# Four scheduling edits in the attention layers of a four-layer transformer block: residual rows by pairs of tiles, the mask row written from another queue, later mask copies, an earlier v tile

## The chip, the cores and the metric

The kernel runs on one core of a Trainium2 chip. A core has a matrix engine (TensorE, PE in the profile, with its weight loads listed apart as PEld), three engines for elementwise work (VectorE or DVE, ScalarE or ACT, GpSimd or POOL) and SyncE (SP), which here only issues DMA transfers. Each engine works through its own instructions in order. PE writes its results to PSUM, from where DVE or ACT has to bring them to the on-chip SBUF; DMA transfers move data between SBUF and device memory, and here also between partitions of SBUF. A DMA is issued from an engine's queue and occupies that engine for the time of the issue only, but an issue can wait for a semaphore, and everything behind it on that engine waits with it.

The metric is device time in microseconds (us) of one launch on this core: the median of several runs.

## The reference

Four layers, A, B, A, B, on an input of 2048 rows of 576 bf16 values; each adds its result to its input.

```python
def _A_ref(x, wqkv, wo):            # D=576, H=32 heads, Dh=18
    W, dil = (8, 2)
    q, k, v = split_heads(x @ wqkv)
    idx = pos[:, None] - (arange(W) * dil)[None, :]      # 8 keys: own row, 2 back, ... 14 back
    logits = einsum('bhsd,bhswd->bhsw', q, k[idx]) * Dh ** -0.5
    logits = where(idx >= 0, logits, -1e9)
    o = einsum('bhsw,bhswd->bhsd', softmax(logits), v[idx])
    return merge_heads(o) @ wo

def _B_ref(x, w_in, w_sp, b_sp, w_out):                  # F=4608
    z = gelu(x @ w_in)
    z1, z2 = z[..., :2304], layernorm(z[..., 2304:])
    g = einsum('ts,bsf->btf', w_sp, z2) + b_sp           # w_sp: 2048 x 2048
    return einsum('bsf,fd->bsd', z1 * g, w_out)

x = x + _A_ref(layernorm(x), A_wqkv, A_wo)
x = x + _B_ref(layernorm(x), B_w_in, B_w_sp, B_b_sp, B_w_out)
...
```

The two lines are run twice, with the same weights.

## The kernel before

**Layout.** The normalised input is kept transposed in `xnT` (features on partitions, 5 pieces of 128, the last one half filled). Queries and keys are wanted with each head on its own 18 partitions of a group of 32: `QK` is 128 partitions (4 heads) x 2 (q and k) x 8 groups x 2064 columns. The 14 partitions that a head leaves free hold the mask: rows of a pattern that repeats every 256 columns, so arranged that the matmul of a key tile with a query tile adds a large negative number wherever a key is not one of the 8 that a query may see. The rows are built once in a small tile (`win_rows`, L123), written to device memory (`win_period`, L174, in the function that the prologue calls as `rows[2]`), read back by four loads into the spread layout (`load_pat`, L176), and copied along the columns by DVE: `fill_window_rows` (L188), four copies of 128x4096 (L197) for each half of 1024 columns.

**Projections.** `VW(t, hh)` (L373) computes half of the v rows of query tile t: five matmuls into a `pv` tile of PSUM and one eviction to `v_ext`. `PG(d, qk, cc)` (L384) computes 128 features of q or k (piece d) for 512 rows (chunk cc): five matmuls into `pp`, one eviction to a staging tile (`stg`, L369 on DVE or L371 on ACT). After the last of the four `PG` of a staging tile (both of q and k, two chunks) come its head moves: 7 to 9 DMAs, one per head, from the staging tile to the partitions of that head in `QK`, dealt in turn to SP and POOL. In the first layer A two of the five staging tiles are lent by `win2a`, a weight tile that is loaded later, so the moves of d=3 and d=4 of the first two chunks appear in the profile as `QK<-win2a`.

**Attention.** A query tile has 112 rows (19 tiles) and is done in two steps of 16 heads (38 steps). `L_mm(s)` (L435): 16 matmuls of 32 rows into two `L_ps` tiles (PSUM tag H, 2 buffers); `EXP(s)` (L444): two exponentials on ACT into `P_sb`; `PV(s)` (L455): 16 matmuls into `O_ps`, then a reciprocal and a multiplication on DVE into `o_t` (L461, L462). After the second step of a tile, SP issues a DMA transpose of `o_t` to `oT` (L467). All of `pv`, `pp`, `O_ps`, `pw` and the transposes `pt` share four PSUM buffers (tag PT).

**Output.** For each of 16 tiles of 128 rows: `XO(i)` (L478) loads the residual rows to `xo`, `WO(i, hh)` (L482) multiplies `oT` by `wo` in two halves (`pw`, L489) and adds `xo` (L492) into `x_new`, `XST` stores it, `LN_STATS` (L500) and `LN_XN` (on POOL, L242 and L245) normalise it for the next layer, `LN_T` has SP transpose it into `xnT`. `xo` has three buffers, `x_new` four.

**Order.** Inside a layer A no scheduler reorders anything: each engine executes its instructions in the order of the code. The loop over steps puts out `L_mm(s+1)`, `EXP(s+1)`, `PV(s)` and then whatever `table` holds for step s: the `PG` of chunks 2 and 3 that are left after six `pre` ones (steps 0 to 12, more than one at some), the v tiles not yet done, weight loads, and the output stages, whose step follows from the tile that they need.

**The opening of the first layer A** is a sequence written out by hand (L572 to L631): `S_` statistics of input tiles on DVE, `E_` adds epsilon to a variance (DVE), `R_` raises it to the power -0.5 (POOL), `A_` normalises (DVE), `T_pe` transposes on PE with a copy on ACT (L567), `T_` transposes by DMA, with `VW` and `PG` between them, then v tiles 4 to 7, the second half of the mask copies, `L_mm(0)`, `EXP(0)` and the six `pre` groups. At its start SP's queue issues the loads of x, `wv`, x, `wqk` (key half, then query half) and x.

The layers B (L714 on) are not touched.

Of the kernel before, what the change touches and what calls it, by code (L numbers as in the profile page):

```python
# [18 lines left out]
P = 128  # L19
D = 576  # L20
# [42 lines left out]
class K:  # L63
# [48 lines left out]
        self.xn_rr = 0  # L112
        self.deferred = []

    def build_window_rows(self, c):

        nc = self.nc
        R = c.tile([P, 2, MR, 16], bf16, name="win_rows")  # L123
        self.pat = self.consts.tile([P, 2, 272], bf16, name="win_pat")
        self.patpad = self.consts.tile([P, PADL], bf16, name="win_patpad")
        n = c.tile([P, 3], i32, name="win_n")
        g = c.tile([P, 3], i32, name="win_g")
        bits = c.tile([P, 5, 3], i32, name="win_bits")
        vf = c.tile([P, 5, 3], f32, name="win_vf")
        uu = c.tile([P, 4, 2], f32, name="win_uu")  # L130
        half = WB / 2
        nc.gpsimd.iota(n[:], pattern=[[1, 3]], base=15, channel_multiplier=1)
# [12 lines left out]
        nc.gpsimd.memset(R[:, 0, 13, :], -2.5 * WB)  # L145
        nc.gpsimd.memset(R[:, 1, 13, :], 1.0)
        one = self.dram.tile([2, MR, 256], bf16, name="win_period")
        for xb in self.xn_bufs:
            nc.gpsimd.memset(xb[:, D:640], 0.0)

        def part0():
            nc.vector.tensor_scalar(out=n[:], in0=n[:], scalar1=15, scalar2=None, op0=ALU.bitwise_and)
            nc.vector.tensor_scalar(out=g[:], in0=n[:], scalar1=1, scalar2=None, op0=ALU.logical_shift_right)
            nc.vector.tensor_tensor(out=g[:], in0=g[:], in1=n[:], op=ALU.bitwise_xor)
            for i in range(4):
                nc.vector.tensor_scalar(out=bits[:, i, :], in0=g[:], scalar1=i, scalar2=1,
                                        op0=ALU.logical_shift_right, op1=ALU.bitwise_and)
            nc.vector.tensor_scalar(out=bits[:, 4, :], in0=n[:], scalar1=1, scalar2=None, op0=ALU.bitwise_and)

        def pads():  # L160
            nc.gpsimd.memset(self.pat[:], 0.0)
            nc.gpsimd.memset(self.patpad[:], 0.0)
            for j in range(4):
                nc.gpsimd.affine_select(out=self.patpad[:], in_=self.patpad[:], compare_op=ALU.not_equal, fill=1.0,
                                        base=-32 * j - 31, pattern=[[0, PADL]], channel_multiplier=1)

        def part1(eng):
            nc.vector.tensor_scalar(out=vf[:], in0=bits[:], scalar1=-2.0, scalar2=1.0, op0=ALU.mult, op1=ALU.add)
            nc.vector.tensor_scalar_mul(out=R[:, :, 0:8, :], in0=R[:, :, 0:8, :], scalar1=vf[:, 4, 1:2])
# [152 lines left out]
    def layer_A(self, li):  # L322
# [17 lines left out]
        oT = main.tile([P, 5, RING * P], bf16, name="oT")  # L340
        sb_cm = tc.tile_pool(name=f"A{li}_sb", bufs=2, reuse_waits="tile")
        sb = sb_cm.__enter__()
        if self.right is None:
            self.open_right()
        R = self.right
# [130 lines left out]
        tails = {}  # L476

        def XO(i):  # L478
            tails[i] = dict(xo=sb.tile([P, D], x_prev_dt, name="xo", tag="xo", bufs=3))
            self.dma(tails[i]["xo"][:], x_prev[i * P:(i + 1) * P, :], eng=nc.sync)  # L480

        def WO(i, hh):  # L482
            st = tails[i]
            if hh == 0:
                st["x"] = sb.tile([P, D], f32, name="x_new", tag="x_new", bufs=4)
            r0 = (i % RING) * P
            pw = self.PT_tile([P, 512], f32, "pw")
            for c in range(5):
                nc.tensor.matmul(pw[:, 0:288], lhsT=oT[:, c, r0:r0 + P], rhs=wo_sb[:, c, hh * 288:(hh + 1) * 288],  # L489
                                 start=(c == 0), stop=(c == 4))  # L490
            hs = slice(hh * 288, (hh + 1) * 288)
            nc.vector.tensor_tensor(out=st["x"][:, hs], in0=pw[:, 0:288], in1=st["xo"][:, hs], op=ALU.add)  # L492
# [17 lines left out]
        if li == 0:  # L510
# [19 lines left out]
            warm = self.PT_tile([P, 512], f32, "warm")  # L530
            for _ in range(46):
                nc.tensor.matmul(warm[:, 0:P], lhsT=self.ident[:], rhs=self.ident[:], start=True, stop=True)
            rows = self.build_window_rows(sb)
            nc.scalar.copy(out=v_ext[:, :, :, DH:DH + 1], in_=self.ones[:, None, None, :].to_broadcast([P, NT, H, 1]))
            rows[0]()
            mvs = sb.tile([P, NS, 2], f32, name="lnx_mv", tag="lnx_mv", bufs=1)
# [6 lines left out]
                        nc.vector.bn_stats(out=st[:, s, :], in_=xts[i][:, s * 288:(s + 1) * 288])  # L543
                    nc.vector.bn_aggr(out=mvs[:, i, :], in_=st[:])

            def E_(i0, n):
                nc.vector.tensor_scalar_add(out=rstds[:, i0:i0 + n], in0=mvs[:, i0:i0 + n, 1], scalar1=EPS)

            def R_(i0, n):
                nc.gpsimd.tensor_tensor(out=rstds[:, i0:i0 + n], in0=rstds[:, i0:i0 + n],  # L550
                                        in1=self.neg_half[:, 0:1].to_broadcast([P, n]), op=ALU.pow)
            xns = {}

            def A_(*tiles):
# [15 lines left out]
                for i in tiles:  # L570
                    self.ln_T(xns.pop(i), i * P, P)
            S_(0)  # L572
            E_(0, 1)
            R_(0, 1)
            S_(1)
            E_(1, 1)
            R_(1, 1)
            A_(0)
            T_pe(0)
            VW(0, 0, False)  # L580
            VW(0, 1, False)
            S_(2)
            A_(1)
            T_pe(1)
            VW(1, 0, False)
            S_(3)
            E_(2, 2)
            R_(2, 2)
            rows[1]()
            setup_bufs(nc.gpsimd)  # L590
            rows[2](nc.scalar)
            A_(2, 3)
            T_pe(2)
            T_pe(3)
            VW(1, 1, False)
            x_load(sb.tile([P, 4, D], bf16, name="x_in3", tag="x_in", bufs=2)[:], 12, 4, nc.sync)
            S_(4, 5)
            E_(4, 2)
            R_(4, 2)
            VW(2, 0, False)  # L600
            VW(2, 1, False)
# [1 line left out]
            A_(4, 5)  # L603
            T_(4, 5)
            S_(7)
            E_(6, 2)
            R_(6, 2)
            S_(8)
            A_(6, 7)
            T_(6, 7)  # L610
            self.load_pat(nc.sync)
            S_(9, 10, 11)
            E_(8, 4)
            R_(8, 4)
            S_(12)
            A_(8, 9, 10, 11)
            T_(8, 9, 10, 11)
            self.fill_window_rows(QK, 0)
            S_(13, 14, 15)
            E_(12, 4)  # L620
            order = [(d, 0) for d in range(4)] + [(d, 1) for d in range(4)] + [(4, 0), (4, 1)]
            for k_, (d, cc) in enumerate(order):
                for qk in ((1, 0) if d < 4 else (0,)):
# [23 lines left out]
        for t in range(nvw0, nvw):  # L647
            for hh in range(2):
                VW(t, hh, li == 0)
        if li == 0:  # L650
            self.fill_window_rows(QK, 1)

        pieces = []

# [12 lines left out]
        PG_END = 14  # L667
        pre, pgs = pgs[:6], pgs[6:]
        for k_, (d, qk, cc) in enumerate(pgs):
            at((k_ * PG_END) // len(pgs), PG, d, qk, cc, True)  # L670
        for t in range(nvw, NT):
            for hh in range(2):
                at(2 * t - 2 + hh, VW, t, hh, 2 * t - 2 + hh >= PG_END and hh == 0)
        for i in range(NS):
            t = -(-(i + 1) * P // QT) - 1
            s = 2 * t + (6 if li == 0 and t < 8 else 5 if t < NT - 5 else 4 if t < NT - 3 else 3)
            at(s - 5, XO, i)
            at(s, WO, i, 0)
            at(s + 1, WO, i, 1)
            at(s + 1, LN_STATS, i)  # L680
            at(s + 2, LN_XN, i)
            at(s + 2, XST, i)
            if i < NS - 1:
                at(s + 4, LN_T, i)
# [8 lines left out]
        at(NST, O_T, NT - 1)  # L693
        L_mm(0)
        EXP(0)
        for d, qk, cc in pre:
            PG(d, qk, cc, li > 0, q2)
        for s in range(NST):
            if s + 1 < NST:
                L_mm(s + 1)  # L700
# [343 lines left out]
```

The softmax here doesn't subtract the row's maximum and nothing guards it: scores larger than these inputs give would overflow.

## Time and profile before

| what | us |
|---|---|
| median of 6 runs (1193.01 to 1197.96) | 1194.18 |
| the profiled execution, by the same clock as the runs | 1196.53 |
| its span in the profile | 1194.8 |
| PE busy in the span | 1172.7 |
| opening, 0 to 24: PE busy | 18.45 |
| projections of the first layer A, 24 to 50: PE busy of 26 | 24.85 |
| its attention loop, 50 to 118: PE busy of 68 | 63.16 |
| first layer B, 118 to 595: PE busy of 477 | 474.42 |
| projections of the second layer A, 595 to 645: PE busy of 50 | 49.68 |
| its attention loop, 645 to 715: PE busy of 70 | 68.38 |
| second layer B, 715 to 1194.8: PE busy of 479.8 | 473.70 |

The stage borders are mine, to the nearest few us; the busy times are the profile's. The loops are full of small groups. In the first one (50 to 118) they are, with the columns line, engine, operation, output<-inputs, shapes, count, then busy time and mean ns of one, then idle time of the engine ahead of them and what ended it:

```profile
L444 ACT ACTIVATE P_sb<-L_ps 128x896 bf16<-128x896 f32 x59 | 50.6, 916 | 16.2 <-PE L_ps L435 15.8
L455 PE MATMUL O_ps<-v_ext,P_sb 128*128 128x19 bf16 x480 | 16.9, 172 | 0.0
L489 PE MATMUL pw<-wo_sb,oT 128*128 128x288 bf16 x100 | 15.5, 286 | 2.7 <-DMA oT<-o_t 1.9 <-DVE o_t L462 0.8
L400 PE MATMUL pp<-xnT,wqk_sb 128*128 128x512 bf16 x54 | 14.5, 378 | 0.3
```

A row of the order of time gives start, duration, engine, line, operation and names, and in brackets how long the engine was idle before it and what it had waited for; SPq, ACTq and POOL L77 are DMA issues (L77 is the helper that issues them all). Here a stretch of SP's queue in the first loop:

```profile
92.24 0.53 SPq L77 DMA_DIRECT2D xo<-in_A_x_dram  x1
92.86 1.20 SPq L249 DMA_TRANSPOSE xnT<-ln_xn  x1
94.11 0.57 SPq L77 DMA_DIRECT2D xres<-x_new  x1
94.79 1.29 SPq L467 DMA_TRANSPOSE oT<-o_t  x1
96.17 1.51 SPq L249 DMA_TRANSPOSE xnT<-ln_xn  x1
```

A stage's row in the table by windows has the window, its length, the busy time and number of instructions of PE, PEld, DVE, ACT and POOL, the granted TensorE clock (1.00 is full speed), the mean busy share of the 16 DMA engines (it can read above 1), and GB/s.

### The profile page before, as it was taken

The numbers are of one execution on the slowest core, as the hardware profiler recorded it, in microseconds if no ns is written. First come the engines' busy times: TensorE is split into PE (matmuls) and PEld (weight loads), VectorE is DVE, ScalarE is ACT, GpSimd is POOL, SyncE is SP. The second block draws the span as 40 slices with busy tenths as digits, with TensorE's granted clock in tenths as the row PEclk, the third lists the DMA queues.
The fourth block names the chain that finished last, engine by engine and source line by source line (L and its number), as shares of the span: only waits on it lengthen the run. The fifth ranks groups of instructions, "written<-read, shape, count | busy, mean of one in ns | idle before, by whom it ended". The sixth has DMA issues, their size and how long they took to land.

```text
span 1194.8 us, 20693 instructions
## 1 busy us (share of the span) xinstructions
PE 1172.7 (98%) x8457; PEld 620.0 (52%) x8554; DVE 545.4 (46%) x1202; ACT 378.7 (32%) x597; POOL 275.1 (23%) x382
## 2 busy tenths in 40 slices
PE   8999999999999999999999999999999999999998
PEld 5566644444444444457755775444444444444676
DVE  8577677333233233244455776763223223233321
ACT  5577677211111111201156786770110110111000
POOL 3677774100000000001153867630000000000000
PEclk9999999999999999999999999999999999999999
DMA  8799891000000000049645799900000000001332
GB/s 193 146 198 225 167 257 35 23 1 12 12 12 12 12 1 12 2 139 294 170 98 120 172 233 221 199 11 12 12 12 1 12 12 12 12 1 30 122 105 73
DMA packets 178791, 101.21 MB, mean 85 GB/s; under 512 B 135039, under 2 KB 160047, under 8 KB 178696
## 3 DMA queue, kind: packets, MB, share of 16 engines
q1 hardware_dynamic: 165400, 78.14, 29.5%
q0 software_dynamic: 6480, 15.99, 5.1%
q10 hardware_dynamic: 6816, 5.77, 1.6%
q8 instruction: 67, 1.10, 0.4%
q14 instruction: 28, 0.23, 0.1%
HBM read 42.39 MB, written 16.53 MB: 49 GB/s over the span
## 4 chain that ended last, share of the span: by engine, by line
PE 93%; DMA 2%; issue 1%; ACT 0%; DVE 0%; DVEq 0%; ACTq 0%
PE pg L878 41%; PE pz L860 12%; PE po L932 12%; PE pz L782 11%; PE pp L400 4%; PE pw L489 3%; PE O_ps L455 3%; PE pv L377 3%; PE L_ps L435 2%; PE pzs L782 1%; DMA oT<-o_t 1%; ACT P_sb L444 0%; DMA QK<-win2a 0%; PE pt L473 0%; DVE ln_st L218 0%
## 5 line engine op out<-in xcount | busy, mean ns | idle before, releaser
L878 PE MATMUL pg<-Wq,Z 128*128 128x512 bf16 x2256 | 500.3, 379 | 2.5
L878 PEld LDWEIGHTS <-Z 128*128 128x128 bf16 x2304 | 225.5, 98 | 271.7
L882 DVE TENSOR_TENSOR g_tmp<-pg,ln_xn 128x512 f32<-128x512 f32 x144 | 99.6, 692 | 428.1 <-PE pg L878 428.1
L872 ACT ACTIVATE z1T<-pz 128x1024 bf16<-128x1024 f32 x72 | 73.7, 1024 | 513.8 <-PE pz L860 513.6
L77 POOL DMA_DIRECT2D wout<-in_B_w_out_dram x4 | 4.2, 1060 | 604.6 <-PE pg L878 604.6
L932 PE MATMUL po<-wout,Z 128*128 128x288 bf16 x1152 | 141.4, 286 | 0.0
L444 ACT ACTIVATE P_sb<-L_ps 128x896 bf16<-128x896 f32 (+1 forms) x152 | 126.7, 887 | 42.3 <-PE L_ps L435 41.5
L860 PE MATMUL pz<-xnT,w 128*128 128x512 bf16 (+1 forms) x630 | 134.4, 380 | 1.6 <-issue 1.6
L932 PEld LDWEIGHTS <-Z 128*128 128x128 bf16 x1152 | 112.7, 98 | 28.8
L782 PEld LDWEIGHTS <-xnT 128*128 128x128 bf16 (+1 forms) x800 | 66.3, 97 | 80.9 <-issue 23.7
L883 DVE TENSOR_TENSOR Z<-g_tmp,z1T 128x512 bf16<-128x512 f32 x144 | 99.7, 692 | 10.8 <-DVE g_tmp L882 1.4
L782 PE MATMUL pz<-win2a,xnT 128*128 128x512 bf16 x366 | 103.5, 380 | 0.8
L860 PEld LDWEIGHTS <-w 128*128 128x128 bf16 (+1 forms) x640 | 51.1, 97 | 80.0 <-issue 27.1
L400 PE MATMUL pp<-xnT,wqk_sb 128*128 128x512 bf16 x341 | 81.0, 379 | 0.9
L796 ACT ACTIVATE zp<-pz 128x1024 bf16<-128x1024 f32 x64 | 65.5, 1024 | 36.7 <-PE pz L782 34.1
L242 POOL TENSOR_SCALAR ln_xn<-x_new,ln_mv,ln_rstd 128x576 bf16<-128x576 f32 x32 | 73.4, 2293 | 2.7
L942 DVE TENSOR_TENSOR x_new<-po,xo 128x288 f32<-128x288 f32 (+1 forms) x64 | 28.8, 455 | 88.0 <-PE po L932 83.7
L782 PE MATMUL pz<-win2b,xnT 128*128 128x512 bf16 (+1 forms) x256 | 65.8, 380 | 0.0
L798 DVE CUSTOM_DVE_ANT_0 Z<-zp 128x1536 bf16<-128x1536 bf16 x32 | 56.5, 1764 | 15.8 <-ACT zp L796 15.6
L377 PE MATMUL pv<-wv_sb,xnT 128*128 128x288 bf16 (+1 forms) x380 | 56.2, 285 | 3.8 <-ACT xnT L567 3.7
L77 POOL DMA_DIRECT2D QK<-stg x81 | 49.8, 619 | 39.8 <-DVE stg L369 13.4
L489 PE MATMUL pw<-wo_sb,oT 128*128 128x288 bf16 x320 | 48.8, 286 | 3.2 <-DMA oT<-o_t 2.4
(111 smaller groups left out, 873.0 us busy)
## 6 DMA issues: line engine op xcount, KB each, us to landing
xres<-x_new SPq DMA_DIRECT2D x48, 288.0 KB
xo<-xres SPq DMA_DIRECT2D x48, 288.0 KB
wout<-in_B_w_out_dram POOLq DMA_DIRECT2D x4, 1296.0 KB, 8.6
w<-in_B_w_in_dram SPq DMA_DIRECT2D x16, 256.0 KB
QK<-stg POOLq DMA_DIRECT2D x53, 72.0 KB, 4.2
QK<-stg SPq DMA_DIRECT2D x41, 72.0 KB
xo<-in_A_x_dram SPq DMA_DIRECT2D x16, 144.0 KB
win2a<-in_B_w_in_dram POOLq DMA_DIRECT2D x6, 288.0 KB, 4.3
```

The costliest lines, as they stand in the source:

```text
L242: e.tensor_scalar(out=xn[:nrows, 0:D], in0=x_t[:nrows, :], scalar1=mv[:nrows, 0:1], scalar2=rstd[:nrows, 0:1], op0=ALU.subtract, op1=ALU.mult)
L377: nc.tensor.matmul(pv[:nk, 0:288], lhsT=self.xnT[:, c, QT * t:QT * t + nk], rhs=wv_sb[:, c, hh * 288:(hh + 1) * 288], start=(c == 0), stop ...
L400: nc.tensor.matmul(pp[:, :], lhsT=w, rhs=self.xnT[:, c, PADL + cc * 512:PADL + (cc + 1) * 512], start=(c == 0), stop=(c == 4))
L444: nc.scalar.activation(out=P_bufs[(2 * s + jp) % 4][:nk, :, :, 0:nq], in_=Lv[:nk, :, :, 0:nq], func=ACT.Exp, scale=scale)
L489: nc.tensor.matmul(pw[:, 0:288], lhsT=oT[:, c, r0:r0 + P], rhs=wo_sb[:, c, hh * 288:(hh + 1) * 288], start=(c == 0), stop=(c == 4))
L782: nc.tensor.matmul(pzvs[ci][:, sub * 512:sub * 512 + w], lhsT=self.xnT[r0:r1, c, PADL + i * P:PADL + (i + 1) * P], rhs=win2(c)[r0:r1, c0 + ...
L860: nc.tensor.matmul(pz1s[q // 2][:, q % 2, :], lhsT=w1[r0:r1, c, sub * P:(sub + 1) * P], rhs=self.xnT[r0:r1, c, PADL + q * 512:PADL + (q + ...
L872: nc.scalar.activation(out=z1T[:, q2 * 512:(q2 + 2) * 512], in_=pz1s[q2 // 2][:, :, :].rearrange("p a b -> p (a b)"), func=ACT.Gelu_apprx_ ...
L878: nc.tensor.matmul(pg[:, :], lhsT=Z[:, jj, i, sub * P:(sub + 1) * P], rhs=Wq[q][:, i, :], start=(i == 0), stop=(i == NS - 1))
L882: nc.vector.tensor_tensor(out=tmp[:], in0=pg[:, :], in1=bsp[:, qs], op=ALU.add)
L883: nc.vector.tensor_tensor(out=uT(jj)[:, sub, qs], in0=tmp[:], in1=z1Ts[jj, sub][:, qs], op=ALU.mult)
L932: nc.tensor.matmul(acc[hh], lhsT=uT(j // 2)[:, j % 2, i * P:(i + 1) * P], rhs=wouts[j // NJH][:, j % NJH, hh * 288:(hh + 1) * 288], start= ...
```

## The change

1. The residual rows come two tiles at a time: `XO(i)` does nothing for an odd i and loads tiles i and i+1 with one DMA for an even i, at the step at which tile i alone was loaded. `xo` has 2 buffers of two tiles in place of 3 of one. The first two `xo` and all four `x_new` tiles are allocated at the start of the layer.
2. The rows of the mask pattern are built in a part of `oT` that is not in use then, in place of a tile of their own, and the write of the pattern to device memory is issued by POOL instead of ACT.
3. In the opening of the first layer A, `E_` is put out together with `R_`, and the first v tile comes after the transposes of tile 1 instead of before them.
4. In the first layer A the second half of the mask copies comes after the fourth `pre` group instead of before `L_mm(0)`; the first four `pre` groups are evicted by DVE instead of ACT.
5. In the first layer A the twelve remaining `PG` go to steps 2 to 13, one each, instead of steps 0 to 12; v tile 8 goes to steps 0 and 1 (evicted by DVE), instead of 14 and 15; the output stages of the tile that needs query tile 9 (tile 7) come one step later.

```diff
-        R = c.tile([P, 2, MR, 16], bf16, name="win_rows")
...
+        x_news = [sb.tile([P, D], f32, name="x_new", tag="x_new", bufs=4) for k_ in range(4)]
+        xos = {k_: sb.tile([P, 2, D], x_prev_dt, name="xo", tag="xo", bufs=2) for k_ in range(2)}
...
         def XO(i):
-            tails[i] = dict(xo=sb.tile([P, D], x_prev_dt, name="xo", tag="xo", bufs=3))
-            self.dma(tails[i]["xo"][:], x_prev[i * P:(i + 1) * P, :], eng=nc.sync)
+            if i % 2 == 0:
+                xo = xos.pop(i // 2, None) or sb.tile([P, 2, D], x_prev_dt, name="xo", tag="xo", bufs=2)
+                self.dma(xo[:], x_prev[i * P:(i + 2) * P, :].rearrange("(a p) d -> p a d", p=P), eng=nc.sync)
+                for k_ in range(2):
+                    tails[i + k_] = dict(xo=xo[:, k_, :])
...
-            rows = self.build_window_rows(sb)
+            nR = 2 * MR * 16
+            rows = self.build_window_rows(
+                sb, oT[:].rearrange("p a b -> p (a b)")[:, 4 * D:4 * D + nR].rearrange("p (a r f) -> p a r f", a=2, r=MR))
...
-            def E_(i0, n):
-                nc.vector.tensor_scalar_add(out=rstds[:, i0:i0 + n], in0=mvs[:, i0:i0 + n, 1], scalar1=EPS)
-
             def R_(i0, n):
-                nc.gpsimd.tensor_tensor(out=rstds[:, i0:i0 + n], in0=rstds[:, i0:i0 + n],
-                                        in1=self.neg_half[:, 0:1].to_broadcast([P, n]), op=ALU.pow)
+                rs = rstds[:, i0:i0 + n]
+                nc.vector.tensor_scalar_add(out=rs, in0=mvs[:, i0:i0 + n, 1], scalar1=EPS)
+                nc.gpsimd.tensor_tensor(out=rs, in0=rs, in1=self.neg_half[:, 0:1].to_broadcast([P, n]), op=ALU.pow)
...
             T_pe(0)
-            VW(0, 0, False)
-            VW(0, 1, False)
             S_(2)
             A_(1)
             T_pe(1)
+            VW(0, 0, False)
+            VW(0, 1, False)
             VW(1, 0, False)
...
-            rows[2](nc.scalar)
+            rows[2](nc.gpsimd)
...
-        if li == 0:
-            self.fill_window_rows(QK, 1)
...
-            at((k_ * PG_END) // len(pgs), PG, d, qk, cc, True)
+            at(2 + k_ if li == 0 else (k_ * PG_END) // len(pgs), PG, d, qk, cc, True)
         for t in range(nvw, NT):
             for hh in range(2):
-                at(2 * t - 2 + hh, VW, t, hh, 2 * t - 2 + hh >= PG_END and hh == 0)
+                if li == 0 and t == nvw:
+                    at(hh, VW, t, hh, True)
+                else:
+                    at(2 * t - 2 + hh, VW, t, hh, 2 * t - 2 + hh >= PG_END and hh == 0)
...
-            s = 2 * t + (6 if li == 0 and t < 8 else 5 if t < NT - 5 else 4 if t < NT - 3 else 3)
+            s = 2 * t + (6 if li == 0 and t < 10 else 5 if t < NT - 5 else 4 if t < NT - 3 else 3)
...
-        for d, qk, cc in pre:
-            PG(d, qk, cc, li > 0, q2)
+        for k_, (d, qk, cc) in enumerate(pre):
+            PG(d, qk, cc, li > 0 or k_ < 4, q2)
+            if li == 0 and k_ == 3:
+                self.fill_window_rows(QK, 1)
```

More of the change, by code (lines that the diff above doesn't have):

```diff
@@ L113, in setup, with build_window_rows @@
         self.deferred = []
-    def build_window_rows(self, c):
+    def build_window_rows(self, c, R):
         nc = self.nc
-        R = c.tile([P, 2, MR, 16], bf16, name="win_rows")
         self.pat = self.consts.tile([P, 2, 272], bf16, name="win_pat")
@@ L484, in WO @@
             if hh == 0:
-                st["x"] = sb.tile([P, D], f32, name="x_new", tag="x_new", bufs=4)
+                st["x"] = x_news[i] if i < 4 else sb.tile([P, D], f32, name="x_new", tag="x_new", bufs=4)
             r0 = (i % RING) * P
@@ L572, in layer_A @@
             S_(0)
-            E_(0, 1)
             R_(0, 1)
             S_(1)
-            E_(1, 1)
             R_(1, 1)
@@ L584, in layer_A @@
             T_pe(1)
+            VW(0, 0, False)
+            VW(0, 1, False)
             VW(1, 0, False)
             S_(3)
-            E_(2, 2)
             R_(2, 2)
@@ L597, in layer_A @@
             S_(4, 5)
-            E_(4, 2)
             R_(4, 2)
@@ L605, in layer_A @@
             S_(7)
-            E_(6, 2)
             R_(6, 2)
@@ L612, in layer_A @@
             S_(9, 10, 11)
-            E_(8, 4)
             R_(8, 4)
@@ L619, in layer_A @@
             S_(13, 14, 15)
-            E_(12, 4)
             order = [(d, 0) for d in range(4)] + [(d, 1) for d in range(4)] + [(4, 0), (4, 1)]
```

## The prediction

> **What bounds the kernel.** First the page's busy line, then TensorE's waits, then the stages that hold them.
>
> ```profile
> PE 1172.7 (98%) x8457; PEld 620.0 (52%) x8554; DVE 545.4 (46%) x1202; ACT 378.7 (32%) x597; POOL 275.1 (23%) x382
> ...
> PE pv L377 <- ACT xnT L567: 3.7, 3, 2.1
> PE pw L489 <- DMA oT<-o_t: 2.4, 3, 1.4
> PE L_ps L435 <- ACT P_sb L444: 2.2, 6, 0.4
> PE L_ps L435 <- DMA QK<-win2a: 1.5, 3, 0.7
> ```
>
> TensorE is busy all but 22 us, so an edit that takes no matmul away can only win idle time. A wait line gives total, times, longest. The table by stage shows where it lies (us, then PE busy):
>
> ```profile
> 0.00:20.00 20.00, 14.46 (x116) 10.56 (x118) 16.95 (x65) 10.82 (x16) 8.68 (x42) 1.00 0.94 239
> 40.00:60.00 20.00, 18.31 (x236) 9.70 (x239) 12.04 (x21) 13.45 (x18) 9.28 (x12) 1.00 0.79 137
> 100.00:120.00 20.00, 17.02 (x332) 12.20 (x332) 13.63 (x42) 14.62 (x20) 14.55 (x17) 1.00 1.10 238
> 680.00:700.00 20.00, 18.98 (x382) 13.88 (x379) 14.83 (x44) 16.88 (x23) 14.66 (x16) 1.00 1.20 232
> ```
>
> Idle: 5.5 us in the opening, 1.7 where attention begins, 3.0 late in the first layer A, 1.0 in the second. The granted clock is 1.00 throughout.
>
> **Opening.** The order of time on ACT and PE:
>
> ```profile
> 11.02 0.40 ACT L371 CAST v_ext<-pv 128x288 bf16<-128x288 f32 x1 [0.88 <-PE pv L377]
> 13.14 0.33 ACTq L77 DMA_DIRECT2D win_period<-win_rows  x1
> 13.52 1.29 ACT L567 COPY xnT<-pt 128x640 bf16<-128x640 bf16 x2 [2.10 <-DVE lnx_mv L544]
> 14.26 1.40 PE L377 MATMUL pv<-wv_sb,xnT 128*128 128x288 bf16 x10 [2.11 <-ACT xnT L567]
> ```
>
> The copies need only transposes that ended at 11.5; the mask write ahead of them in ACT's queue is what waits. In the built program the transfers of SP and ACT take eight completion counters in turn (POOL's have eight others), and an issue waits until the last transfer on its counter has landed: here the key half of wqk. Moved to POOL, the write holds nobody there: POOL is through with its memsets at 12.34, its next operation (the pow at 13.65) awaits DVE, and its one issue costs 0.6 (head move) to 1.06 (the 1.3 MB wout row). The readers (load_pat, SP, 21.08) are far off. Putting the transposes of tile 1 ahead of the first v tile removes the 0.81 us wait at 10.19 as well, so PE could start wqk 2.1 earlier. But its second group reads the query half. By bytes in queue order, key half (2.36 MB) landed near 13.1, x tiles 8 to 11 (3.76 MB) at 16.88; the query half (3.10 MB) falls at 15.1. PE read it at 16.6. Gain 1.4; bounds 0.3 (SP's second transpose, behind the query half's counter, starts at 16.3) and 2.1.
>
> [...]
>
> **Head moves.** The first attention half needs the moves of d=0, 1 and the first two of d=2, the second (L_mm(1)) the moves of d=3 and 4, which POOL issues last:
>
> ```profile
> 41.35 5.49 POOL L77 DMA_DIRECT2D QK<-win2a  x5 [0.28 <-DMA QK<-stg]
> 41.62 4.62 DVE L197 COPY QK<-win_pat 128x4096 bf16<-128x4096 bf16 x4
> ...
> 50.42 0.09 PEld L435 LDWEIGHTS <-QK 32*128 32x128 bf16 x1 [0.85 <-DMA QK<-win2a]
> ...
> QK<-win2a POOLq DMA_DIRECT2D x1, 72.0 KB, 6.1
> ...
> QK<-win2a POOLq DMA_DIRECT2D x2, 36.0 KB, 4.0
> ```
>
> Five issues take 5.49 us where the median is 0.587, that is 2.94. Singly they end at 42.94, 44.07, 45.21, 46.35 and 46.84; the copies end at 42.84, 43.98, 45.11 and 46.24: each issue comes free 0.1 us after a mask copy. The change puts those four copies behind four pp evictions, at about 46.2. Without them the fifth issue is held by its counter only: the transfer eight before it, issued at 38.73 and 6.1 us on the way, lands at 44.8. POOL's chain (no gap from 28.60 to 41.07) starts with the first stg, up to 1.4 sooner; but half 0's copies run from 24.49 to 29.12 and slow its first two moves to some 1.1 each, so 0.7 is left. Fifth issue 44.1 instead of 46.33; last landing, 4.0 to 4.5 later, 48.1 to 48.6 instead of 50.4. PE comes to L_mm(1) at 46.7 instead of 48.05 and resumes at 48.3 instead of 50.4: **gain 2.1**, the opening's 1.4 included. Bounds: 1.1 (POOL starts no sooner, 4.5 us: 49.3) and 2.9 (landing in 3.4, the least of the five before). SP's moves from 28.58 to 42.0 stay, behind transposes that DVE times.
>
> What the copies now delay: 46.2 + 4.6 = 50.8 for the first reciprocal. Four PSUM buffers cover that; PE needs the first again at PV(2), near 52. If the cover fails, up to 1 us. Four pp evictions of 0.69 go to DVE, four of 0.59 leave ACT: both idle there. Merging E_ with R_ changes no order that anyone awaits; the pow of tiles 12 to 15 stands behind POOL's moves before and after. Storing the rows in oT and allocating tiles early issue nothing.
>
> **Loop of the first layer A.** From one PV to the next I read 1.92 and 2.22 in turn with a pp (mean 2.07), 2.53 with pp and pw, 1.92 with neither, 2.23 with pw alone. Steps 0 to 15 took 35.4 before. After: two with pv (ACT's two P_sb, 1.73, set the pace: 1.85), six with pp, six with both, two with pw (2.1): 35.5. **0**, within 0.4. PG of chunk 3 at step 2 falls near 52, after its transposes (issued by 47.3).
>
> But the last head moves (d=4) now leave at step 13, not 12. PE reaches PV(13) at 77.3 and the eviction ends near 79.8; SP, behind the transpose of o_t 6, issues four moves at 0.78 from about 81.8, the last landing 3.5 later at 88.4; L_mm(19) wants them at 87.5. **Loss 0.9**; bounds 0 (landing in 2.8, the quickest move) and 2.0 (4.5).
>
> **Output tiles.** SP is full from 55 to 118: the transpose of o_t 9, ready at 93.8, is issued at 99.47. So pw waits: 1.39 (tile 7), 0.48, and 0.78 put down to o_t: 2.65 in all. Pair loads drop four xo issues by then, 4 x 0.5 = 2.0 us of SP; its first head moves start 1.2 later. Tile 7 also moves one step (2.1) on. I take the 1.39 and half of the rest as won, 2.0, less 0.7 for a step that loses its pw and becomes ACT's: **gain 1.3**; bounds 0 (the DMA share, 1.10, sets the pace: the bytes are the same) and 2.65.
>
> **Second layer A.** Only pairs (f32) change; no new buffer wait: pair i still waits for add i-3. Two waits, 0.49 (oT) and 0.40 (P_sb, not touched). **Gain 0.2**; bounds +0.5 and -1.2 (288 KB more ahead of one transpose at 240 GB/s).
>
> **Sum.** 2.1 + 0 - 0.9 + 1.3 + 0.2 = 2.7. The profiled execution took 1196.53 (span 1194.8 and 1.73 around it), 2.35 above the median of six: 1193.8 for it, 1191.5 for the median.
>
> **Rivals.** (1) *SP and the DMA engines keep the pace*: what PE wins by 50 us it gives back at L_mm(19) and the pw waits, since the bytes and most issues stay. For it: DMA share 1.10 at 100 to 120. Against: every xo dropped leaves the full queue. Gain 2.1 - 2.0 + 0.6 + 0 = 0.7: 1193.5. (2) *Pair loads in front of transposes*, in the second layer A: an even tile's load of 576 KB stands ahead of an o_t transpose that pw awaits, while the share is 1.2. Price 1.2 each at pairs 8 to 14, 4.8, and the output term falls away: 1194.18 - 1.2 + 4.8 = 1197.8, slower. It eats the whole gain from 0.34 us a pair over eight pairs (2.7 / 8). Against: only one pw wait there now. (3) *The copies are not what slows POOL* but the counters: then the five issues stay, the change does not do what it says, and 0.3 to 1 is left at L_mm(1): 2.7 - 1.5 = 1.2: 1193.0. Against: the ends 0.1 behind each copy.
>
> **Chances.** Forecast 0.55, rivals 0.23 (1), 0.12 (2), 0.10 (3). The forecast's own range is 1189.5 to 1191.8; the whole reaches to rivals 1 and 3 and stops at 1195.0, leaving most of rival 2 and gains above 4.7 out. 0.2% (2.4 us) is about what this kernel's measurement can tell from no change: faster 0.55, same 0.33, slower 0.12.
>
> **What would show it.** Five issues in under 3.6 us before 45; L_mm(1) through by 48.6; no idle PE at 12 to 14; mask copies from 46; a QK wait near 87; pw waits under 1 us in 95 to 115. Wrong if L_mm(1) still ends past 50, or the second layer A shows pw waits above 2.

## The result, and the profile after

The changed kernel takes 1197.30 us (median of 38 runs, 1193.85 to 1200.80); the kernel before, run beside it, 1195.92 (median of 78). The ratio is 1.0013, with a 95% interval of 1.0007 to 1.0019: 1.6 us slower where 2.7 us of gain had been forecast. That is inside the 0.2% that were called no change, and clear of zero on the wrong side. (The profiled execution of one experiment, e5, ran at a granted clock of 0.95 from end to end, so no profile of it is read below.)

The profiled execution took 1197.59 us (span 1195.8). From its page, the busy line and the granted clock in 40 slices:

```profile
PE 1175.2 (98%) x8457; PEld 621.8 (52%) x8554; DVE 547.8 (46%) x1207; ACT 376.0 (31%) x592; POOL 273.5 (23%) x383
...
PEclk9998999999999999999999999999999999999999
```

And TensorE's waits (total, times, longest):

```profile
PE L_ps L436 <- DMA QK<-stg: 4.6, 1, 4.6
PE pw L493 <- issue: 2.4, 2, 1.7
...
PE L_ps L436 <- DMA QK<-win2a: 0.2, 1, 0.2
```

The waits that the change aimed at are nearly gone: no pv waits for `xnT`, `QK<-win2a` is down from 1.5 to 0.2 us, no pw waits for `oT` (not a proof of part 1, as e10 will show). One wait of 4.6 us is new, and PE's busy time is 2.5 us longer although the page lists the same 8457 matmuls: one digit of the granted clock is 8. The table by stage (us, then PE, PEld, DVE, ACT, POOL, clock, DMA share, GB/s) shows where:

```profile
0.00:20.00 20.00, 17.56 (x129) 12.16 (x131) 18.11 (x68) 12.49 (x19) 9.26 (x43) 1.00 1.00 243
40.00:60.00 20.00, 19.58 (x283) 10.65 (x284) 15.52 (x28) 13.76 (x17) 6.00 (x12) 1.00 0.70 137
80.00:100.00 20.00, 13.54 (x235) 9.52 (x232) 9.81 (x29) 9.98 (x14) 13.87 (x17) 0.83 1.16 174
100.00:120.00 20.00, 19.02 (x375) 14.09 (x373) 15.59 (x48) 16.55 (x23) 14.26 (x15) 1.00 1.19 225
```

Idle PE in the opening fell from 5.5 to 2.4 us, where attention begins from 1.7 to 0.4, late in the layer from 3.0 to 1.0, in the second layer A from 1.0 to 0.5. All of it and more is lost between 80 and 100: 6.5 us idle, at a mean clock of 0.83. The order of time on PE there:

```profile
84.35 0.77 PE L378 MATMUL pv<-wv_sb,xnT 128*128 128x288 bf16 x5
84.96 0.29 PE L493 MATMUL pw<-wo_sb,oT 128*128 128x288 bf16 x1
86.98 0.65 PE L493 MATMUL pw<-wo_sb,oT 128*128 128x288 bf16 x4 [1.74 <-issue]
87.56 0.32 PE L436 MATMUL L_ps<-QK 32*128 32x112 bf16 x6
92.50 1.17 PE L436 MATMUL L_ps<-QK 32*128 32x112 bf16 x10 [4.62 <-DMA QK<-stg]
93.60 0.60 PE L456 MATMUL O_ps<-v_ext,P_sb 128*128 128x19 bf16 x16
94.05 1.36 PE L378 MATMUL pv<-wv_sb,xnT 128*128 128x288 bf16 x5
```

In the kernel before, nothing waits there:

```profile
89.83 0.51 PE L435 MATMUL L_ps<-QK 32*128 32x112 bf16 x16
90.27 0.56 PE L455 MATMUL O_ps<-v_ext,P_sb 128*128 128x19 bf16 x16
```

In the changed kernel L_mm(19) starts, finds the last head moves (d=4) missing, and waits. Afterwards the same five pv matmuls take 1.36 us instead of 0.77. Counted by the start of PV, the loop is ahead of the kernel before by 4.0 us at PV(1) (48.48 against 52.50) and by 4.2 at PV(17) (83.93 against 88.09); at PV(18) it is 3.3 us behind (93.60 against 90.27). So one place took 7.5 us: the 4.62, the 1.74 and the slower clock.

The head moves at the start of attention came as forecast, and sooner: L_mm(1) is through at 46.73, where 48.6 was asked for. POOL's last moves, in the order of time (POOL, DVE, PE):

```profile
37.70 3.56 POOL L77 DMA_DIRECT2D QK<-win2a  x6
41.51 1.55 POOL L77 DMA_DIRECT2D QK<-win2a  x3 [0.24 <-DMA QK<-stg]
...
44.38 4.62 DVE L196 COPY QK<-win_pat 128x4096 bf16<-128x4096 bf16 x4
...
46.30 0.43 PE L436 MATMUL L_ps<-QK 32*128 32x112 bf16 x2 [0.18 <-DMA QK<-win2a]
```

Before, five issues took 5.49 us, the first four of them ending 0.1 us behind a mask copy each; now the last three take 1.55, and the copies run behind them.

### The profile page after: what moved, and what is told of

The parts are those of the page before. It is cut to its first block, busy times and chain, and to the rows that moved or that the text cites. A ratio compares the mean times of both kernels' runs of the same rounds, so it can differ in the third digit from the quotient of the medians.

```text
span 1195.8 us, 20663 instructions
## 1 busy us (share of the span) xinstructions
PE 1175.2 (98%) x8457; PEld 621.8 (52%) x8554; DVE 547.8 (46%) x1207; ACT 376.0 (31%) x592; POOL 273.5 (23%) x383
## 4 chain that ended last, share of the span: by engine, by line
PE 95%; DMA 1%; POOL 1%; issue 1%; DVE 1%; ACT 1%; SPq 0%
PE pg L878 41%; PE pz L860 12%; PE po L932 12%; PE pz L782 11%; PE pp L401 5%; PE pw L493 3%; PE pv L378 3%; PE O_ps L456 3%; PE L_ps L436 2%; PE pzs L782 1%; POOL QK L77 1%; DMA QK<-stg 1%; ACT P_sb L445 1%; DMA QK<-win2a 0%; DVE ln_st L549 0%
## 5 line engine op out<-in xcount | busy, mean ns | idle before, releaser
L883 DVE TENSOR_TENSOR Z<-g_tmp,z1T 128x512 bf16<-128x512 f32 x144 | 99.7, 692 | 10.1 <-DVE g_tmp L882 0.5
```

The source lines that it names most:

```text
L883: nc.vector.tensor_tensor(out=uT(jj)[:, sub, qs], in0=tmp[:], in1=z1Ts[jj, sub][:, qs], op=ALU.mult)
```

## The experiments

All ratios are to the kernel before, on the same chip, each with its 95% interval; medians are of 12 runs (5 for e4). Runs of one kernel spread over some 6 us and each kernel has one profile, so a wait read from it is a sample.

**The first question: which part brought the wait?** Part 5 undone, pairs undone, the six weight loads taken out of the stretch, and part 5 alone.

```diff
# e1, against the changed kernel
-            at(2 + k_ if li == 0 else (k_ * PG_END) // len(pgs), PG, d, qk, cc, True)
+            at((k_ * PG_END) // len(pgs), PG, d, qk, cc, True)
-                if li == 0 and t == nvw:
-                    at(hh, VW, t, hh, True)
-                else:
-                    at(2 * t - 2 + hh, VW, ...)
+                at(2 * t - 2 + hh, VW, ...)
-            s = 2 * t + (6 if li == 0 and t < 10 else ...)
+            s = 2 * t + (6 if li == 0 and t < 8 else ...)
```


> The changed kernel with part 5 alone undone (remaining PG at steps 0 to 12 again, v tile 8 at 14 and 15, tile 7's output not shifted). Theory 'late by order': in the changed kernel PE waits 4.62 us at L_mm(19) because the last head moves (d=4) are put out a step later; with the old order they leave 3 to 5 us earlier, the wait falls under 1 us, the granted clock stays at 1.00, and the time falls 5 to 7 us below the changed kernel (about 4 below the kernel before). Rival 'slow moves': the moves are late because they take 11.1 us to land among the weight and residual loads, whatever step puts them out; then the wait stays above 3 us and the time within 1.5 us of the changed kernel.

Measured: 1193.29 us, ratio 0.9977 (0.9965 to 0.9989). No wait for `QK<-stg` at L_mm(19); 4.3 us below the changed kernel by the ratios (0.0036 of 1195.9), somewhat less than the 5 to 7 expected. The rest of the change is a gain, and part 5 eats it.

```diff
# e2, against the changed kernel
             if i % 2 == 0:
                 xo = xos.pop(...)
-                self.dma(xo[:], x_prev[i * P:(i + 2) * P, :].rearrange(...), eng=nc.sync)
                 for k_ in range(2):
                     tails[i + k_] = dict(xo=xo[:, k_, :])
+            self.dma(tails[i]["xo"], x_prev[i * P:(i + 1) * P, :], eng=nc.sync)
```


> The changed kernel with one residual tile per transfer again (two for each pair, at the old steps; the allocation stays). If the 288 KB pair loads ahead of the head moves in SP's queue are what makes them land late, the wait at L_mm(19) falls under 2 us and the time falls by 3 to 6 us. If they are not ('late by order' and 'slow moves' by weights alike), the wait stays within 1 us of 4.62, SP has 8 more issues of 0.5 us in the first layer A, and the time is the changed kernel's or up to 1.5 us more.

Measured: 1197.62 us, ratio 1.0014 (1.0002 to 1.0026), the changed kernel's time. The wait is 3.2 us and 0.4 more, with head moves that land in 5.9 us at the most. Pair loads don't cause it, and landing times as long as the changed kernel's 11.1 us are not needed for it.

```diff
# e3, against the changed kernel
-                at(5 + 2 * k_, f)          # six win2a loads
+                at(k_ // 2, f)
```


> The changed kernel with the six win2a loads (288 KB each, POOL) at steps 0 to 2 in place of 5 to 15: into the stretch 47 to 55, where the DMA share is 0.17 to 0.98, and off the head moves. 'Slow moves': head moves of chunks 2 and 3 land in 5 us or less again (median was 6.7, longest 11.2), no wait above 1 us at L_mm(19), clock 1.00, time 5 to 8 us below the changed kernel. 'Late by order': the last moves still leave at 80 to 84 and the wait stays above 3 us, the time within 1.5 us.

Measured: 1194.34 us, ratio 0.9990 (0.9979 to 1.0001); head moves land in 5.6 us or less (4.2 in the median), and three short waits are left at L_mm(19), 1.4 us in all. Neither expectation fits whole: landing got quicker, the time fell by some 2.8 us, half of what the theory of slow moves asked for.

```diff
# e4: the diff of e1 the other way round, on the kernel before
```


> The kernel before with part 5 alone (PG at steps 2 to 13, v tile 8 at 0 and 1, tile 7's output a step later). 'Late by order': the last moves leave a step later against the same consumer, a wait of 3 to 5 us at L_mm(19), time 4 to 7 us above the kernel before. If the wait needs the earlier start of the loop as well (PE 3.9 us ahead while SP's and POOL's queues are not), the wait is under 1.5 us and the time within 1.5 us of the kernel before.

Measured: 1200.04 us, ratio 1.0036 (1.0024 to 1.0048): 4.3 us slower, with a wait at the same place:

```profile
94.43 1.20 PE L435 MATMUL L_ps<-QK 32*128 32x112 bf16 x10 [4.96 <-DMA QK<-stg]
```

Part 5 needs none of the other edits to do its damage; alone and taken out of the whole it gives the same 4.3 us.

**The second question: what are the parts worth?** e5 and e12 change the changed kernel, e11 the kernel before; the others undo or move one part more in e1.

```diff
# e5, against the changed kernel: PG steps alone undone
-            at(2 + k_ if li == 0 else (k_ * PG_END) // len(pgs), PG, d, qk, cc, True)
+            at((k_ * PG_END) // len(pgs), PG, d, qk, cc, True)
```


> The changed kernel with only the PG of chunks 2 and 3 back at steps 0 to 12; v tile 8 stays at 0 and 1, tile 7's output a step later. If the PG steps are what made part 5 dear (last moves a step, about 2.2 us, later), the wait for QK<-stg at L_mm(19) falls under 1.5 us and the time is within 0.15% of e1 (1193.3), 3 to 5 us below the changed kernel. If moving v tile 8 or the outputs is what costs (two PT users more in the early steps, the later pw ones bunched), the time stays within 1.5 us of the changed kernel.

Measured: 1195.14 us, ratio 0.9995 (0.9984 to 1.0006), 2.2 us below the changed kernel and 2.2 above e1: between the two expectations.

```diff
# e6, against e1
+        if li == 0:
+            self.fill_window_rows(QK, 1)           # before L_mm(0)
...
-            PG(d, qk, cc, li > 0 or k_ < 4, q2)
-            if li == 0 and k_ == 3:
-                self.fill_window_rows(QK, 1)
+            PG(d, qk, cc, li > 0, q2)
```


> e1 with part 4 undone too (mask copies of the second half before L_mm(0) again, all pre groups evicted by ACT). If the copies hold POOL's last five issues, these take 5 us or more again, L_mm(1) ends 1 to 2 us later than in e1, and the time rises by 1.0 to 2.0 us. If POOL's issues are held by the counters anyway, the time stays within 0.6 us of e1.

Measured: 1194.40 us, ratio 0.9994 (0.9984 to 1.0005), 2.0 us above e1. POOL's last nine issues in e6, in the order of time:

```profile
37.73 7.62 POOL L77 DMA_DIRECT2D QK<-win2a  x9
```

And in e1:

```profile
37.85 1.17 POOL L77 DMA_DIRECT2D QK<-win2a  x2
39.34 0.59 POOL L77 DMA_DIRECT2D QK<-win2a  x1 [0.32 <-DMA QK<-stg]
40.95 0.59 POOL L77 DMA_DIRECT2D QK<-win2a  x1 [1.01 <-DMA QK<-stg]
41.69 2.81 POOL L77 DMA_DIRECT2D QK<-win2a  x5 [0.16 <-issue]
```

Nine take 7.62 us behind the copies; without them the issues are 0.6 us each and what holds them is, as forecast, the landing of an earlier transfer. Even so POOL is through at 44.5 in e1 and at 45.4 in e6: the copies cost 0.9 us at POOL, and L_mm(1) ends 1.0 us later (PV(0) starts at 48.79 instead of 47.77).

```diff
# e7, against e1
-            rows[2](nc.gpsimd)
+            rows[2](nc.scalar)
# and the two calls VW(0, 0), VW(0, 1) again right behind T_pe(0)
```


> e1 with the opening undone (mask write from ACT again, first v tile before the transposes of tile 1). If the write waits for the key half of wqk in every execution, as in the trace of before (2.1 us of idle PE), the time rises by 1.4 to 2.7 us. If that wait depends on when the load lands (in e4, with the same opening, the write left at 11.12 without waiting), the trace shows it in some runs only, and the time rises by 0.3 to 1.0 us.

Measured: 1193.42 us, ratio 0.9978 (0.9967 to 0.9990): the opening is worth nothing that shows, though the two intervals together leave some 2 us either way. The write of the mask from ACT in e7:

```profile
11.11 0.34 ACTq L77 DMA_DIRECT2D win_period<-oT  x1
```

It leaves at 11.11, without the two us of waiting that the profile of before shows (13.14). In e4 it left at 11.12 and in e11 at 11.53. Of four executions with the write on ACT, one had the long wait. What the new opening does win, PE has no use for: PE starts with q and k at 12.77 in e1 and at 13.47 in e7, but at L_mm(0) e1 waits for head moves that POOL starts no sooner (26.92 in e1, 26.64 in e7), and e7 does not:

```profile
40.71 0.22 PE L436 MATMUL L_ps<-QK 32*128 32x112 bf16 x1 [1.38 <-DMA QK<-stg]
```

That is e1, in the order of time on PE; e7's row at 39.11 has its 16 matmuls without a gap.

```diff
# e8, against e1: the edit of e3
```


> e1 with the six win2a loads at steps 0 to 2 instead of 5 to 15. If the DMA engines are what delays the transposes and moves of steps 8 to 28, the waits for oT<-o_t (3.8 us in e1) and QK<-stg (1.4) shrink together by 2 us or more and the time falls by 1 to 3 us. If SP's queue sets these waits (its issues are the same), the time stays within 0.8 us of e1; it is worse if the 1.7 MB now delays the transfers of wo and the first transposes.

Measured: 1197.62 us, ratio 1.0012 (0.9997 to 1.0026): 4 us slower than e1, though the same edit helped the changed kernel. POOL's queue shows what changes: the second load waits for the head moves that read the lent tiles, and four loads then go out in the middle of the moves of the next chunk.

```profile
48.50 0.59 POOL L77 DMA_DIRECT2D win2a<-in_B_w_in_dram  x1 [0.55 <-DMA QK<-win2a]
54.39 2.38 POOL L77 DMA_DIRECT2D QK<-stg  x4 [5.29 <-DVE stg L370]
56.76 2.23 POOL L77 DMA_DIRECT2D win2a<-in_B_w_in_dram  x4
```

In its profile PE runs at half clock in three stretches of 3.4 us (from 48.2, 65.2 and 75.5), where e1 has one; at about 1.7 us each, the two more are most of the 4 us. Why e8 has more of them and e3 gained was not followed further.

```diff
# e9, against e1: tile 7's output a step later (t < 10 again)
# e10, against e1: the edit of e2
# e11, on the kernel before: part 4 alone, the lines of e6 the other way round
# e12, against the changed kernel
-            at(2 + k_ if li == 0 ...
+            at(3 + k_ if li == 0 ...
```


> The changed kernel with PG steps and v tile 8 both as before; of part 5 only the output of tile 7 a step later remains. Theory 'margin': what counts is the PE work between the last PG and L_mm(19), 11.2 us in the kernel before, 8.4 in e4; moving v tile 8 away takes 1.4 us of it, tile 7's output is behind L_mm(19) and takes none. Then this kernel is e1's equal (ratio 0.9965 to 0.9989, no clear difference). Rival: the shifted output is what kept e5 2 us above e1; then the ratio stays near e5's 0.9995.

Measured: 1192.78 us, ratio 0.9972 (0.9959 to 0.9984), e1's equal. The later output costs nothing.

> e1 with one residual tile per transfer. If pairs win SP time at the output tiles (prediction: 1.3 us in the first layer A, 0.2 in the second), the time rises by 0.8 to 2.0 us, and pw waits and the 0.5 us wait of the second layer A come back. If e1's gain of 2.7 us is the fill's 2.0 and little else, the time rises by 0 to 0.7.

Measured: 1194.40 us, ratio 0.9991 (0.9977 to 1.0005), 1.7 us above e1 by the ratios. In the second layer A, pw waits for `oT` of 1.2 us in all are back, where e1 has none; the two longest:

```profile
693.92 0.79 PE L493 MATMUL pw<-wo_sb,oT 128*128 128x288 bf16 x5 [0.58 <-DMA oT<-o_t]
698.76 0.79 PE L493 MATMUL pw<-wo_sb,oT 128*128 128x288 bf16 x5 [0.37 <-DMA oT<-o_t]
```

In the first layer A it is the other way round: such waits come to 1.6 us in e10, and to 3.8 in e1, which has the pairs. Its rows:

```profile
91.56 0.79 PE L493 MATMUL pw<-wo_sb,oT 128*128 128x288 bf16 x5 [2.19 <-DMA oT<-o_t]
109.19 0.79 PE L493 MATMUL pw<-wo_sb,oT 128*128 128x288 bf16 x5 [1.65 <-DMA oT<-o_t]
```

Nor do the missing waits of the changed kernel speak for the pairs: e4, with single loads, has none behind its stall at L_mm(19) either.

> The kernel before with part 4 alone (mask copies after the fourth pre group, these four evicted by DVE). If the parts add up (e6 against e1 gives 2.0 for it), 1.4 to 2.6 us below the kernel before. If the fill only pays together with pairs or the opening, within 0.8 us of it.

Measured: 1195.04 us, ratio 0.9991 (0.9979 to 1.0002): 1.1 us, short of the 2.0 from e6 but not clear of it.

> The changed kernel with PG at steps 3 to 14, one step later again. 'Margin': 2.2 us less between the last PG and L_mm(19), so the wait there grows by 1.5 to 3 us beyond the changed kernel's 3.2 to 4.6 and the time by 1.5 to 4 us. Rival 'SP phase': the changed kernel's moves are late because step 13 has the transpose of o_t ahead of them in SP's queue and step 14 has none; then the wait stays as it is or shrinks, and the time stays within 1 us.

Measured: 1196.32 us, ratio 0.9999 (0.9984 to 1.0013). Another step later is not worse, and in its profile the wait is 2.0 us. So the PE work between the last PG and L_mm(19) does not settle it alone. The rival that looks at SP's queue has the number right, but not its reason: in this profile too, a transpose of `o_t` and one of `xnT` go out between the last PG and its moves.

**The third question: what holds the last moves?** The last PG put ahead of PV(13), v tile 8 alone moved back, and all PG by step 11.

```diff
# e13, against the changed kernel
+            if li > 0 or k_ < len(pgs) - 1:
                 at(2 + k_ if li == 0 ...
...
+            if li == 0 and s == 13:
+                PG(*pgs[-1], True)
             PV(s)
# e14, against the changed kernel: the VW lines of e1 alone
# e15, against e9: at(k_ if li == 0 ...), the last PG ahead of PV(11) as in e13
```


> The changed kernel with the last PG of step 13 put out ahead of PV(13), so that its head moves stand ahead of the transpose of o_t 6 in SP's queue; nothing else. 'SP phase': the last moves leave SP 2 to 4 us earlier, the wait for QK<-stg at L_mm(19) falls under 2 us and the time by 1.5 to 4 us below the changed kernel. 'Margin' alone: the PG moves by one PV (0.4 us), the wait stays above 3 us, the time within 1 us.

Measured: 1195.88 us, ratio 1.0000 (0.9986 to 1.0015), 1.6 us below the changed kernel, at the lower end of what was asked and not clear of it by the intervals; the waits at L_mm(19) are 1.6, 0.3 and 0.2 us.

> The changed kernel with v tile 8 back at steps 14 and 15; PG stays at 2 to 13. 'Margin': 1.4 us of PE work returns between the last PG and L_mm(19), the wait there shrinks by 1 to 2 us, the time by 1 to 2.5 us. If the margin isn't what counts: within 0.7 us of the changed kernel.

Measured: 1198.56 us, ratio 1.0018 (1.0003 to 1.0033): taking v tile 8 back alone wins nothing. The run does not clear the tile, though: without it steps 0 and 1 hold neither a PG nor a v tile, and from 51.4 to 54.8 the profile has a stretch at half clock that the changed kernel's has not. (e5 stands 2.8 us above e9, with v tile 8 as the only difference and intervals that just touch; what that tile costs with the old PG steps stays open.)

> e9 (PG at 0 to 12, v tile 8 at 14 and 15) with PG at steps 0 to 11, one each, the last ahead of PV(11). If what is left of the wait at L_mm(19) in e9 (1.2 us) is the last moves' lateness, it is gone and the time is 0.5 to 1.5 us below e9 (ratio 0.996 to 0.997). If SP's queue then only delays the transposes of o_t instead, the pw waits grow by as much and the time is e9's.

Measured: 1193.29 us, ratio 0.9979 (0.9966 to 0.9992). No matmul waits for `QK<-stg` in its profile; the time is e1's and e9's. The 1.2 us that the expectation put at L_mm(19) in e9 lie at L_mm(0) (its row is at 40.41), and L_mm(19) had nothing left to win.

Across the profiles one quantity sorts the kernels: the time from the end of SP's last head-move issue to the moment at which PE starts L_mm(19) (negative where PE comes first). It has two parts, the time that SP takes from the end of the last PG's matmuls to its last move, and the time that PE takes from there to L_mm(19) (11.2 us in the kernel before, 8.5 in e4). The table also counts the DMA transposes that SP issues between the last PG and the moves.

| kernels | last PG | transposes between | us from PG to SP's last move | us from there to PE at L_mm(19) | wait at L_mm(19), us |
|---|---|---|---|---|---|
| before, e1, e6, e7, e8, e9, e10, e11 | step 12 | 1 | 4.8 to 6.6 | 4.7 to 6.5 | none at L_mm(19) |
| e15 | step 11, ahead of PV | 0 | 4.9 | 8.3 | none |
| after, e2, e3, e4, e14 | step 13 | 2 | 7.1, 10.1, 9.7, 10.0, 10.6 | 3.4, -1.6, -1.1, -1.5, 1.0 | 4.6, 3.6, 1.4, 5.0, 3.9 |
| e13 | step 13, ahead of PV | 1 | 6.1 | 2.9 | 2.1 |
| e12 | step 14 | 2 | 7.9 | -1.0 | 2.0 |

With 4.7 us or more nothing waits, with 3.4 or less PE does. How long it waits depends on the landing as well: e3's moves leave as late as e4's, and its waits come to 1.4 us.

SP's queue shows what lies in between. In e4, in the order of time:

```profile
83.45 1.23 SPq L249 DMA_TRANSPOSE xnT<-ln_xn  x1
84.74 0.57 SPq L77 DMA_DIRECT2D xres<-x_new  x1
85.41 2.02 SPq L467 DMA_TRANSPOSE oT<-o_t  x1
87.52 3.10 SPq L77 DMA_DIRECT2D QK<-stg  x4
```

In the kernel before, with the last PG at step 12:

```profile
78.45 1.57 SPq L467 DMA_TRANSPOSE oT<-o_t  x1
80.12 0.52 SPq L77 DMA_DIRECT2D xo<-in_A_x_dram  x1
80.73 3.10 SPq L77 DMA_DIRECT2D QK<-stg  x4
```

In e4 PE is through with the last PG at 80.63, but the moves leave from 87.52: step 13 ends a query tile, so its transpose of `o_t` stands ahead of them, and ahead of that a transpose of `xnT` and a store that step 12 had put out. At step 12 only the transpose of the tile before and one load come first. In the changed kernel itself SP was quicker (its moves left by 84.14), but POOL's moves took 11 us to land; for SP's the profile lists no landing. POOL's issues with their count, KB and us to landing, in the changed kernel:

```profile
QK<-stg POOLq DMA_DIRECT2D x3, 36.0 KB, 11.1
```

The same moves in the kernel before:

```profile
QK<-stg POOLq DMA_DIRECT2D x3, 36.0 KB, 3.9
```

So the moves can be late in two ways, by SP's queue (e2, e4, e14) and by slow landing (the changed kernel; 8.8 us in e14); with the last PG at step 13 either one reaches PE. What makes a landing slow was not found: e1 has landings of 6.5 to 7.5 us for the same moves, without a wait.

## Why the prediction was wrong

**L_mm(19), the step that failed.** The prediction saw that the last moves leave a step later and that L_mm(19) would wait for them, and priced it at 0.9 us with bounds 0 and 2.0. Part 5 costs 4.3 us, twice over (e4, 2.9 to 5.7 by its interval, and e1 against the changed kernel). The sum had SP start the four moves 2 us after the eviction, behind the transpose of `o_t` 6 alone. It did not list what step 12 leaves in SP's queue, a transpose of `xnT` and a store, which wait ahead of that transpose: the issues end about 10 us after the PG in four of five kernels, where the forecast's own times (PV(13) at 77.3, last issue near 85) leave some 6. Its landing of 3.5 us, bounds 2.8 and 4.5, was too narrow as well: POOL's share of these moves took 11.1 us in the changed kernel and 5.7 in e4. Not all of the 4.3 us is traced to the moves: taking only the PG steps back wins 2.2 of them (e5), the rest comes when v tile 8 goes back too (e1, e9), and what that tile does there stays open. The lead that the earlier edits win did not add to it, as far as the intervals tell: e4, without them, loses the same 4.3 us. The first rival, that the gain is given back at L_mm(19), had the right place, but its reason (the bytes and most issues stay) was not the one: e1, with the same bytes, keeps the gain.

**The clock, a term that was not in the sum.** The profile of before has 1.00 in every stage, and the sum took idle time as the whole price of a wait. A window of the changed kernel behind the wait (PE busy is the first number after the length; the clock is the third from the end):

```profile
92.00:96.00 4.00, 3.40 (x35) 2.21 (x36) 1.18 (x3) 1.73 (x2) 2.52 (x3) 0.50 1.19 247
```

PE works on from 92.5 at half the clock until about 96.2, so some 1.9 us (half of 3.7) come on top of the wait.

**The opening.** Of the 2.1 us at L_mm(1), 1.4 were put down to the mask write on ACT. The step was read from one execution: the wait was there, but in three other executions of that order the write left at 11.11 to 11.53, and undoing the move costs nothing that shows (e7 against e1). The 0.7 us that remain are waited for again at L_mm(0) in e1, a consumer that the step left out. By these profiles the term was near 0, below its lower bound of 0.3; the intervals alone do not exclude 1.4. (The sum of the step itself is 16.6 less 15.1, which is 1.5.)

**Head moves.** Without the opening's 1.4 the term was 0.7. By e6 it is worth 2.0, by e11 1.1; that the copies hold the issues is shown by the issue times (0.85 us each over the nine in e6, about 0.6 in e1). It seems sized too small, though e11's interval takes in 0.7, and the clock may be a part of it: in e6 the stall at L_mm(1) is followed by half clock from 50.0 to 53.4. That the copies merely delay a reciprocal, covered by the PSUM buffers, held: in the changed kernel the first reciprocal starts at 48.92, and PE has no wait from 46.73 to 60.

**Output tiles and second layer A.** 1.3 and 0.2 were forecast; e10 gives 1.7 for both together. The size fits, though the interval of e10 alone overlaps that of e1; the place does not. The waits for `oT` that pairs remove show in the second layer A (1.2 us in e10, none in e1), while in the first one e1 waits longer than e10 and than the kernel before (1.9). So the 1.3 us of the first layer A are not shown, and that the total came out right is in part luck. What supports a gain of both the pairs and the head moves is that four kernels with both parts (e1, e7, e9, e15) lie at 0.9972 to 0.9979, and three that lack one of them (e6, e10, e11) at 0.9991 to 0.9994.

**The loop's steps** priced at 0 were fine up to there: from PV(1) to PV(17) the changed kernel takes 35.45 us (48.48 to 83.93), the one before 35.59. (In the kernel before, the twelve remaining PG stand one each at steps 0 to 12, with none at step 6; no step has more than one.) Rival 2, pair loads ahead of transposes, fell (e2, e10); its 1197.8 is near the measured median only because the kernel before came out 1.7 us higher over 78 runs than over the first six. Rival 3, the counters alone, fell with e6.

Put together: 2.0 for the head moves, 1.7 for the pairs, 0 for the opening, against 4.3 for part 5, is 0.6 us slower; measured, 1.6. The best version is the change without its new PG and v steps: 1192.78 us in e9, 0.28% below the kernel before (0.16 to 0.41%).

## What to carry to other kernels

When a step is moved that issues DMAs, write out the queue of the issuing engine from the step before to the step after, with every transpose, store and load: here one step later meant one transpose more ahead of the moves, and in four of five kernels 3 to 6 us. Compare the time of the last issue plus the longest landing seen, not the usual one, with the time at which the consumer comes. A gain upstream can be lost again at the next consumer whose producer did not speed up, as the opening's was at L_mm(0). And a wait in one profile is a sample: before pricing its removal, see whether the same wait is in another execution.

## What the runs showed of the hardware

The price of a stall can include the clock behind it. Half clock (0.50) came in stretches of 3.4 us, or twice or three times that: 89.4 to 96.2 in the changed kernel, 91.3 to 101.5 in e4, and one stretch each after waits of 1.4 to 2.6 us in e1, e3, e10, e11 and e12. In e1 the 3.4 us before and after such an edge:

```profile
107.17:110.58 3.41, 1.76 (x38) 1.05 (x37) 1.44 (x5) 1.38 (x4) 2.80 (x3) 1.00 1.09 173
110.58:114.00 3.42, 3.42 (x47) 2.08 (x44) 1.92 (x6) 1.72 (x3) 0.81 (x2) 0.50 1.17 238
```

A wait of 1.65 us, with PE busy for half of the stretch, was followed by 3.4 us at half clock, which cost about another 1.7. In e10 a wait of 1.38 us was followed by such a stretch, while waits of 2.19 us in e1 (ahead of 91.56), of 2.0 in e9 and of 1.39 in the kernel before drew no drop: the length of a wait alone does not tell whether the clock falls, and what does was not shown. In e12 a stretch at half clock followed 3.4 us in which no wait was longer than 0.44 us:

```profile
52.03:55.44 3.41, 2.60 (x68) 2.02 (x68) 3.01 (x9) 3.08 (x5) 0.00 (x0) 1.00 0.02 6
55.44:58.85 3.41, 3.19 (x44) 1.43 (x40) 1.03 (x3) 1.42 (x2) 0.00 (x0) 0.50 0.35 69
```

The 1.74 us before 86.98 in the changed kernel lie between the first and the second of a group of five matmuls, and are put down to the issue of instructions; at the same time (85 to 86) the DMA engines moved 4 GB/s. e14 has such a gap of 1.04 us, at 128 GB/s (90 to 91). The kernel before has none in pw. The cause was not tested.
